# Top-k attention and a gated MLP: the place of a score copy in ScalarE's order, and the slots in which q and k are loaded and prepared

## The chip, the cores and the metric

The kernel runs on one core of a Trainium2 chip. Its engines are TensorE (matmuls, PE in the profile; weight loads are listed as PEld), VectorE (DVE), ScalarE (ACT), GpSimd (POOL) and SyncE (SP), which here issues nearly all DMAs. Each works through its own list of instructions in order, and semaphores hold an instruction until what it needs is there. The metric is the device time of one execution in microseconds (us).

## The reference: what is computed

```python
scores = 1/sqrt(64) * q @ k.T               # q, k, v: 8 batches, 8 heads, 576 x 64, fp32
kth    = 32nd largest of each row
scores = where(scores >= kth, scores, -1e9)
attn   = exp(scores - max) / (sum + 1e-9)
x      = (attn @ v), heads side by side     # 4608 x 512
h      = x @ w_in                           # 512 x 2048
out    = (h * sigmoid(1.702 * h)) @ w_out   # 2048 x 512
```

Scores of 576 columns for 36,864 rows (8 x 8 x 576), a cut at the 32nd largest of each row, softmax over what is left, values, and then an MLP with a gate on the 4608 rows of x.

## The kernel before

**Slots.** Attention is cut into 144 slots, 18 to a batch. A slot is 128 query rows for a pair of heads; a batch has four pairs of heads and four full blocks of 128 rows for each (16 slots), and the last 64 rows of two pairs share a slot (2 "ends" slots). Both heads of a slot lie side by side in tiles of 2 x 576.

**The way of one slot m**, by function and line:

- `scores(m)`, L295, PE: scores into two PSUM tiles `s_ps` (there are two such buffers, so one slot's scores fill both). `copy_scores(m)`, L307, ACT: scaled, into the SBUF tile `sc`. It frees `s_ps`.
- `pair_up(m)`, L336, DVE, and L339, L349, POOL: the larger (`greater`) and the smaller (`lesser`) of columns k and k + 288. `pair_up(m)` is the 15th operation of the search of slot m - 1.
- `find(m)`, DVE: the search for the 32nd largest, 23 operations: MAX8 (L366, 8 largest of 288) and MATCH_REPLACE8 (L369) on `greater`, then `pair_up(m + 1)`, then two MAX8, two MATCH_REPLACE8 and two MAX8 on `lesser`, a merge (L373) and the cut (L378).
- `mask(m)`, L423, ACT, two instructions: needs the cut, and drives all below it far down. `exps(m)`, L431, ACT: exponentials and their sums `den`. Both together are `exponentials(m)`.
- `invert(m)`, L439 and L441, DVE: 1 / den. It is put into the search of the next slot, `find(m + 1)`, after a numbered operation. `normalize(m)`, L454, POOL: two multiplications by it.
- `split(m)`, L490, ACT: the 32-bit exponentials as two planes of 16 bits, written over `sc`; a DMA (L492, SP) brings them to DRAM as `rows`. `turn_by_dma(m)`, L498, SP: a transposing DMA brings them back as `pt`.
- `values_at(m)`, L557, PE: `pt` times v, into the PSUM tile `o`. `x_of`, L571 (L574 for ends slots), ACT: into the resident x (`xT`). When a block of 128 rows has all its heads it is ready for the MLP.

**The MLP** has 36 blocks of 128 rows and goes in units of 512 columns of PSUM: `hidden` (L618, PE, into `ph`; four chunks of one block, "x 128", or two chunks of two blocks, "x 256"), `tanh` (L640 and a copy L643, ACT), `gate` (L652, L653, POOL), `project` (L673, PE, into `po`), and when a block has all 16 chunks an eviction `ob` (L681, ACT) and a DMA to the output. `hidden` does nothing when no block is ready.

**The order** is written out by hand. `opening` and `slot(n)` do slots 0 to 12 and round the weights to what the matmuls take. From slot 13 on, `two_slots(n)` (n odd) does two slots in one call, and after the last one `last_slot` does what is left of the MLP. This text calls one such call a pair. In `two_slots(n)` from n = 17 on, ScalarE gets, in this order:

1. `mask(n - 1)`, `exps(n - 1)`; in a preparing pair then the copy into halves (L246, below)
2. `tanh` of the first hidden unit, `split(n - 1)`
3. `mask(n)`, `copy_scores(n + 2)`, `exps(n)`, `x_of`, evictions
4. `copy_scores(n + 3)`, `split(n)`, `tanh` of the second unit, evictions

TensorE gets: hidden, project, `scores(n + 2)` ("first scores"), values of slots n - 3 and n - 2, `scores(n + 3)` ("second scores"), hidden, project. VectorE gets `find(n)` with `invert(n - 1)` in it, and `find(n + 1)` with `invert(n)` in it. Calls 13 and 15 put `scores(n + 2)` and its copy first.

**Loading and preparing q and k.** A table `later` holds what is due in which slot. For a pair of heads hp of batch b, `load` brings q (three DMAs on SP: L184 twice, L187) and k (three more) into one tile of two buffers. From batch 2 on `prepare_by_dma` has ScalarE copy them into 16-bit halves (L246; the tile comes from the pool that also holds the exponentials), four DMAs write them to DRAM (L250 twice, L254, L255), and a transposing DMA (L259, issued behind the one of L498) brings `qT` and `kT`. For batch 1 `prepare_by_pe` does it with transposes on PE: the main parts (L217, copied by ACT at L218), and as `second_part` the ends (`prepare_ends`, L222, copied at L223 and L225). These functions run only in the first slot of a pair, behind step 1 above. `FETCH` and `READY` give the slots of loading and preparing relative to the first slot of the batch, one number for each hp. v is loaded (`load_v`, L198, L206, three DMAs) in the slots `VALUES`.

In `two_slots`, the work of `todo[0]` that is not preparing is issued behind `split(n - 1)` and ahead of its transposing DMA; that of `todo[1]` behind `split(n)` and ahead of its own.

Of the kernel before, what the change touches and what calls it, by code (L numbers as in the profile page):

```python
# [30 lines left out]
def kernel(  # L31
# [250 lines left out]
    PER = N // B  # L282
# [61 lines left out]
    def pair_rest():  # L344

        while unpaired:
            n = unpaired.pop()
            whole, b = lesser[n][:].bitcast(I32), st[n]["sc"][:, :, HALF:S]
            nc.gpsimd.tensor_tensor(out=whole, in0=whole, in1=b.bitcast(I32), op=ALU.add)  # L349
# [44 lines left out]
    def lows(n):  # L394

        top, cut = st[n]["top"], st[n]["cut"]
        low = st[n]["low"] = small.tile([P, 2], F32, name="low")
        for i in range(2):
            nc.gpsimd.tensor_scalar(
                low[:, i : i + 1], cut[:, i : i + 1], top[:, i, TOPK : TOPK + 1], -1.0, op0=ALU.add, op1=ALU.mult  # L400
            )
# [11 lines left out]
    def exponentials(n, between=lambda: None):  # L413

        mask(n)
        between()
        exps(n)

    def mask(n):

        sc, cut = st[n]["sc"], st[n]["cut"]
        for i in range(2):
            nc.scalar.activation(sc[:, i, :], sc[:, i, :], AF.Prelu, bias=cut[:, i : i + 1], alpha=HUGE)  # L423

    def exps(n):

        sc, low = st[n]["sc"], st[n]["low"]
        pr = st[n]["pr"] = prp.tile([P, 2 * S], F32, name="pr")
        den = st[n]["den"] = small.tile([P, 2], F32, name="den")
        for i in range(2):  # L430
            nc.scalar.activation(  # L431
                pr[:, i * S : (i + 1) * S], sc[:, i, :], AF.Exp, bias=low[:, i : i + 1],
                accum_out=den[:, i : i + 1],
            )

    def invert(n):

        some = small.tile([P, 2], F32, name="some", tag="sums")
        nc.vector.tensor_scalar_add(some[:], st[n]["den"][:], 1e-9)  # L439
        rden = st[n]["rden"] = small.tile([P, 2], F32, name="rden", tag="inverse")  # L440
        nc.vector.reciprocal(rden[:], some[:])  # L441
# [158 lines left out]
    to_gate, gated, to_project = [], [], []  # L600

    def hidden(into=None):
        if not ready:
            return
        blocks = ready[:2]
        many = len(blocks)
        fs = blocks[0].left[: G // many]
        first, step = min(x.place for x in blocks), abs(blocks[0].place - blocks[-1].place) or 1
        blocks = sorted(blocks, key=lambda x: x.place)
        if many > 1 or pos["other"] or "ps_h" in in_use:  # L610
            pos["rest"] = 2
        elif pos["rest"]:
            pos["rest"] -= 1
        into = ps_t if pos["rest"] else into
        ph = (into or ps_h).tile([P, G * P], F32, name="ph", tag="tp" if into else "ph")
        for i, f in enumerate(fs):
            for c in range(CC):
                nc.tensor.matmul(  # L618
                    ph[:, i * many * P : (i + 1) * many * P],
                    lhsT=win[:, c, f * P : (f + 1) * P],  # L620
                    rhs=xs[:, first : first + step * (many - 1) + 1 : step, c, :],
                    start=(c == 0),
                    stop=(c == CC - 1),
                )
        to_gate.append((ph, fs, blocks))
        for x in blocks:
            x.left = [f for f in x.left if f not in fs]
        if many > 1:
            pos["other"] = True
        while ready and not ready[0].left:  # L630
            free.append(ready.pop(0).place)
            if len(ready) < 1 or len(ready[0].left) == FC:
                pos["other"] = False
# [13 lines left out]
    def gate(aside):  # L647
        if not gated:
            return
        th, h, g, blocks = gated.pop(0)  # L650
        if aside:
            nc.gpsimd.tensor_scalar(th[:], th[:], 1.0, 1.0, op0=ALU.add, op1=ALU.mult)  # L652
            nc.gpsimd.tensor_tensor(out=th[:], in0=th[:], in1=h[:], op=ALU.mult)  # L653
        else:
            nc.vector.scalar_tensor_tensor(
                out=th[:], in0=th[:], scalar=1.0, in1=h[:], op0=ALU.add, op1=ALU.mult
            )
        to_project.append((th, g, blocks))
# [43 lines left out]
    def at(n, fn, *args):  # L702
        later.setdefault(n, []).append((fn, args))
# [1 line left out]

    READY = (-13, -11, -5, -3)
    READY_1 = (-5, -3, -1, 1)
    FETCH = (-17, -15, -9, -7)  # L710
    FETCH_1 = (-11, -9, -4, -2)
    VALUES = (0, 1, 2, 3)
    by_slot = dict(enumerate([2, 2, 3, 3, 3, 3, 3, 3, 3, 3, 2, 2]))
# [11 lines left out]
            at(hp - 2, prepare, name, 0, hp)  # L725
    for b in range(1, B):
        for hp in range(NP):
            at(b * PER + (FETCH if b > 1 else FETCH_1)[hp], load_both, b, hp)
            if b > 1:
                at(b * PER + READY[hp], prepare_by_dma, b, hp)  # L730
            else:
                at(b * PER + READY_1[hp], prepare_by_pe, b, hp)
            at(b * PER + VALUES[hp], load_v, b, hp)
    unfinished = []
# [3 lines left out]
    def finish_one():  # L738
        unfinished.pop(0)()

    def may_project(waiting):

        return len(to_project) > waiting and len(finished) >= NG * CC + to_project[0][1][-1] + 1
# [62 lines left out]
    def bring_all():  # L806

        waiting = len(ready)
        while put_off:
            put_off.pop(0)()  # L810
        if len(ready) > waiting:
            hidden()
# [90 lines left out]
    def two_slots(n):  # L903

        preparing = prepare_by_dma, prepare_by_pe
        todo = [later.pop(m, []) for m in (n, n + 1)]
        live = lambda m: 0 <= m < N
        aside = n < N
        opens = n == SETTLED + 1
        ahead = n < SETTLED + 4  # L910
        assert not any(fn in preparing for fn, _ in todo[1])

        def begin(some):
            for fn, args in some:
                if fn not in preparing:
                    fn(*args)

        def prepare_some():
            for fn, args in todo[0]:
                if fn in preparing:  # L920
                    fn(*args)

        def find(m):
            for i, op in enumerate(topk_of_pairs(m) if live(m) else [lambda: None] * 23):
                op()
                if i == (20 if m % 2 else 18) and live(m - 1):
                    invert(m - 1)
                if i > 1 and unfinished:
                    finish_one()

        def measure(m):
            if live(m):
                lows(m)
            pair_rest()
            gate(aside)

        def project_one():
            if may_project(0):
                project(True)

        if opens:
            bounds(n - 1)
            gate(aside)
        if ahead:
            scores(n + 2)
        if opens:
            bring_all()
        if live(n - 1):
            exponentials(n - 1)
        if ahead:  # L950
            copy_scores(n + 2)
        if opens:
            leave_all()
            tanh(aside)
        prepare_some()
        hidden(ps_t if opens else None)
        while second_part:
            second_part.pop()()
        project_one()
        find(n)  # L960
        if live(n - 1):
            normalize(n - 1)
        tanh(aside)
        measure(n)
        if live(n - 1):
            split(n - 1)
        begin(todo[0])
        if live(n):
            mask(n)
        held = [m for m in (n - 3, n - 2) if live(m) and "rows" in st[m]]  # L970
        if live(n + 2) and not ahead:
            scores(n + 2)
            copy_scores(n + 2)
        o = ps_t.tile([P, 2, P], F32, name="o", tag="tp") if held else None
        for i, m in enumerate(held):
            values_at(m, o[:, i, :])
        if live(n - 1):
            turn_by_dma(n - 1)
        while turns:
            turns.pop(0)()  # L980
        if live(n + 3):
            scores(n + 3)
        if live(n):
            exps(n)
        if held:
            x_of(held, o)
        leave_all()
        hidden(ps_t)
        if live(n + 3):
            copy_scores(n + 3)  # L990
        find(n + 1)
        if live(n):
            normalize(n)
            split(n)
        begin(todo[1])
        if live(n):
            turn_by_dma(n)
        tanh(aside)
        measure(n + 1)
        project_one()  # L1000
        leave_all()
# [39 lines left out]
```

## Time and profile before

| | us |
|---|---|
| median of 3 runs (lowest, highest) | 1469.7 (1468.23, 1469.85) |
| the profiled execution | 1469.86 |
| its span, first to last instruction | 1468.0 |
| busy: PE, DVE, ACT, POOL | 1428.0, 1337.2, 1154.8, 970.8 |
| slots 13 to 143, by VectorE's searches | from 157.7 to 1396.7 |

The profile shows one execution. Its page gives the busy time of each engine, 40 slices of the span, the chain of work that ended last, and groups of instructions with their count, mean length and the idle time ahead of them. Behind the page stands the trace, which answers with waits (who waited for whom: us in total, times, longest), with a timeline (start, length, engine, line, operation, tiles and shapes, count of instructions merged; in brackets the idle time ahead and what ended it), and with the granted clock of TensorE for any stretch. Two things matter in reading it. Matmuls are pipelined and their ends modelled, so one matmul's row may overlap the next and a waiting TensorE can look busy: differences of starts are safer than lengths. And a float32 matmul has two rows.

Four ranges can be told apart: the opening and slots 0 to 12 (to about 158 us), pairs 13 to 19 with batch 1's preparation on PE (to about 231 us), the steady pairs of 18.8 to 19.8 us (to about 1397 us), and the rest of the MLP on PE, to the end.

### The profile page before, as it was taken

The numbers are of one execution on the slowest core, as the hardware profiler recorded it, in microseconds if no ns is written. First come the engines' busy times: TensorE is split into PE (matmuls) and PEld (weight loads), VectorE is DVE, ScalarE is ACT, GpSimd is POOL, SyncE is SP. The second block draws the span as 40 slices with busy tenths as digits, with TensorE's granted clock in tenths as the row PEclk, the third lists the DMA queues.
The fourth block names the chain that finished last, engine by engine and source line by source line (L and its number), as shares of the span: only waits on it lengthen the run. The fifth ranks groups of instructions, "written<-read, shape, count | busy, mean of one in ns | idle before, by whom it ended". The sixth has DMA issues, their size and how long they took to land. (4 is left out here: it accounts for less than half of the span.)

```text
span 1468.0 us, 29154 instructions
## 1 busy us (share of the span) xinstructions
PE 1428.0 (97%) x9564; PEld 1006.4 (69%) x9564; DVE 1337.2 (91%) x4672; ACT 1154.8 (79%) x1865; POOL 970.8 (66%) x1171
## 2 busy tenths in 40 slices
PE   7789989999999999999999999999999999999998
PEld 5667746777666667777666667777666667777665
DVE  7999999999999999999999999999999999999910
ACT  6998787878788887878888787888878787778730
POOL 3777666676676776666767667667677666677610
PEclk8899999999999999999999999999999999999999
DMA  7452266767677676776678676776768776644530
GB/s 220 142 156 73 64 169 172 203 170 190 160 196 191 181 176 181 199 183 171 173 189 191 180 180 169 203 185 173 186 175 189 179 192 169 165 131 130 136 88 15
DMA packets 516312, 242.04 MB, mean 165 GB/s; under 512 B 452672, under 2 KB 490560, under 8 KB 516160
## 3 DMA queue, kind: packets, MB, share of 16 engines
q1 hardware_dynamic: 515728, 239.89, 62.8%
q8 instruction: 75, 1.23, 0.4%
q14 instruction: 77, 0.63, 0.1%
q10 hardware_dynamic: 432, 0.30, 0.1%
HBM read 45.09 MB, written 102.24 MB: 100 GB/s over the span
## 5 line engine op out<-in xcount | busy, mean ns | idle before, releaser
L618 PEld LDWEIGHTS ph<-xT,win 128*128 128x128 f32 x3520 | 484.7, 191 | 89.0 <-issue 52.6
L618 PE MATMUL ph<-xT,win 128*128 128x128 f32 (+1 forms) x3520 | 538.0, 309 | 3.8 <-ACT xT L574 2.9
L673 PE MATMUL po<-wout,th 128*128 128x512 f32 x1152 | 522.3, 596 | 0.0
L490 ACT COPY sc<-pr 128x2304 uint16<-128x2304 uint16 x132 | 279.0, 2113 | 153.8 <-POOL pr L454 153.7
L673 PEld LDWEIGHTS po<-wout,th 128*128 128x128 f32 x1152 | 214.8, 192 | 214.5 <-issue 209.0
L366 DVE MAX8 top<-left 128x8 f32<-128x288 f32 x792 | 320.9, 446 | 0.0
L339 POOL TENSOR_TENSOR lesser<-sc,greater 128x576 int32<-128x576 int32 x132 | 186.3, 1411 | 195.2 <-DVE greater L336 194.5
L454 POOL TENSOR_SCALAR pr<-pr,rden 128x576 f32<-128x576 f32 x264 | 194.1, 748 | 125.8 <-DVE top L373 85.9
L369 DVE MATCH_REPLACE8 left<-top,left 128x288 f32<-128x288 f32 x528 | 229.6, 442 | 0.0
L431 ACT ACTIVATE pr<-sc,low 128x576 f32<-128x576 f32 x288 | 219.6, 767 | 0.0
L366 DVE MAX8 top<-lesser 128x8 f32<-128x288 f32 x528 | 213.7, 446 | 0.0
L423 ACT ACTIVATE sc<-sc,cut 128x576 f32<-128x576 f32 x288 | 207.4, 770 | 6.5 <-POOL cut L410 3.8
L295 PE MATMUL s_ps<-qk_t 64*128 64x288 f32 (+1 forms) x1280 | 190.3, 433 | 0.2 <-ACT qk_t L218 0.2
L349 POOL TENSOR_TENSOR lesser<-lesser,sc 128x576 int32<-128x576 int32 x132 | 186.5, 1413 | 0.2
L307 ACT ACTIVATE sc<-s_ps 128x576 f32<-128x576 f32 x288 | 170.3, 644 | 4.8 <-PE s_ps L295 3.4
L653 POOL TENSOR_TENSOR th<-th,h 128x512 f32<-128x512 f32 x129 | 165.3, 1282 | 10.8
L295 PEld LDWEIGHTS s_ps<-qk_t 64*128 64x128 f32 (+1 forms) x1280 | 106.2, 178 | 80.1 <-issue 57.8
L640 ACT ACTIVATE th<-ph 128x512 f32<-128x512 f32 x144 | 85.5, 594 | 76.0 <-PE ph L618 72.1
L557 PE MATMUL o<-pt,v_l 128*64 128x128 f32 (+1 forms) x2368 | 143.5, 264 | 0.0
L557 PEld LDWEIGHTS o<-pt,v_l 128*64 128x64 f32 x2368 | 119.8, 137 | 26.9 <-issue 18.4
L336 DVE TENSOR_TENSOR greater<-sc 128x576 f32<-128x576 f32 x132 | 99.8, 756 | 40.0 <-ACT sc L307 40.0
L652 POOL TENSOR_SCALAR th<-th 128x512 f32<-128x512 f32 x129 | 80.0, 620 | 57.7 <-ACT th L640 57.7
(78 smaller groups left out, 1386.6 us busy)
## 6 DMA issues: line engine op xcount, KB each, us to landing
rows<-sc SPq DMA_DIRECT2D x132, 576.0 KB, 3.2
qk_rows<-halves SPq DMA_DIRECT2D x48, 256.0 KB, 2.8
qk_l<-in_q_dram SPq DMA_DIRECT2D x64, 128.0 KB, 3.3
raw<-in_moe_w_in_dram SPq DMA_DIRECT2D x16, 512.0 KB, 4.6
v_l<-in_v_dram SPq DMA_DIRECT2D x32, 256.0 KB, 3.7
raw<-in_moe_w_out_dram SPq DMA_DIRECT2D x16, 512.0 KB, 3.5
out_dram<-ob SPq DMA_DIRECT2D x32, 256.0 KB, 2.9
qk_l<-in_k_dram SPq DMA_DIRECT2D x62, 128.0 KB, 3.0
```

What stands on the lines that cost most here:

```text
L295: nc.tensor.matmul(ps[i][rows, c, 0:HALF], lhsT=qT[b, hps[p]][on, cols], rhs=kT[b, hps[p]][on, FIRST[i] + c * HALF : FIRST[i] + (c + 1) * ...
L339: nc.gpsimd.tensor_tensor(out=whole, in0=a.bitcast(I32), in1=greater[n][:].bitcast(I32), op=ALU.subtract)
L349: nc.gpsimd.tensor_tensor(out=whole, in0=whole, in1=b.bitcast(I32), op=ALU.add)
L366: nc.vector.max(found(r, i, True), src[:, i, :])
L369: nc.vector.match_replace(to[:, i, :], found(r, i), src[:, i, :], LOWEST)
L423: nc.scalar.activation(sc[:, i, :], sc[:, i, :], AF.Prelu, bias=cut[:, i : i + 1], alpha=HUGE)
L431: nc.scalar.activation(pr[:, i * S : (i + 1) * S], sc[:, i, :], AF.Exp, bias=low[:, i : i + 1], accum_out=den[:, i : i + 1],)
L454: nc.gpsimd.tensor_scalar(pr[:, i, :], pr[:, i, :], st[n]["rden"][:, i : i + 1], 1.0, op0=ALU.mult, op1=ALU.mult)
L490: nc.scalar.copy(out=halves, in_=pr[:].bitcast(U16).rearrange("p (k h) -> p h k", h=2))
L557: nc.tensor.matmul(o[j * D : (j + 1) * D, cols], lhsT=main[:, j, c, :] if c < NF else tail[:, j, :], rhs=pt[:, MAIN[j] + c if c < NF else ...
L618: nc.tensor.matmul(ph[:, i * many * P : (i + 1) * many * P], lhsT=win[:, c, f * P : (f + 1) * P], rhs=xs[:, first : first + step * (many - ...
L673: nc.tensor.matmul(x.po[:], lhsT=gT[:, i * P : (i + 1) * P], rhs=wout[:, f, :], start=(x.done == 0), stop=(x.done == FC - 1))
```

## The change

ScalarE's step 3 becomes `copy_scores(n + 2)`, `mask(n)`, `exps(n)`: the copy of the first scores is issued ahead of the mask of the second slot. (In calls 13 and 15, where the copy stands earlier anyway, the order on ScalarE stays.)

`READY` goes from -13, -11, -5, -3 to -13, -9, -5, -1, so that between two preparing pairs there is always another pair. `FETCH` goes to -17, -15, -11, -7, and for batches from 2 on q is loaded in that slot and k in the next one (`FETCH[hp] + 1`, the second slot of the same pair). Batch 1 keeps its slots.

`invert(m - 1)` in `find(m)`: before, behind operation 20 for odd m (first slot of a pair) and 18 for even m. After, behind operation 18, and 20 only for even m in a pair in which something is prepared (`busy`). Between operations 18 and 20 stand two MAX8.

When the first `hidden` of a call had nothing to do, `project_one` runs ahead of `second_part` instead of behind it.

```diff
-    READY = (-13, -11, -5, -3)
+    READY = (-13, -9, -5, -1)
...
-    FETCH = (-17, -15, -9, -7)
+    FETCH = (-17, -15, -11, -7)
...
         for hp in range(NP):
-            at(b * PER + (FETCH if b > 1 else FETCH_1)[hp], load_both, b, hp)
             if b > 1:
+                for i, name in enumerate("qk"):
+                    at(b * PER + FETCH[hp] + i, load, name, b, hp)
                 at(b * PER + READY[hp], prepare_by_dma, b, hp)
             else:
+                at(b * PER + FETCH_1[hp], load_both, b, hp)
                 at(b * PER + READY_1[hp], prepare_by_pe, b, hp)
...
+        busy = any(fn in preparing for fn, _ in todo[0])
...
-                if i == (20 if m % 2 else 18) and live(m - 1):
+                if i == (20 if busy and m % 2 == 0 else 18) and live(m - 1):
                     invert(m - 1)
...
+        units = len(to_gate)
         hidden(ps_t if opens else None)
+        if len(to_gate) == units:
+            project_one()
         while second_part:
             second_part.pop()()
-        project_one()
+        if len(to_gate) > units:
+            project_one()
         find(n)
...
         begin(todo[0])
-        if live(n):
-            mask(n)
         held = [m for m in (n - 3, n - 2) if live(m) and "rows" in st[m]]
         if live(n + 2) and not ahead:
             scores(n + 2)
             copy_scores(n + 2)
...
         if live(n + 3):
             scores(n + 3)
         if live(n):
-            exps(n)
+            exponentials(n)
```

## The prediction

> **What bounds the kernel now.** I read the page's first part, then the waits by engine, then TensorE's own rows of one pair of slots in the timeline. The page leaves two candidates:
>
> ```profile
> PE 1428.0 (97%) x9564; PEld 1006.4 (69%) x9564; DVE 1337.2 (91%) x4672; ACT 1154.8 (79%) x1865; POOL 970.8 (66%) x1171
> ```
>
> The list of waits seems to name VectorE: once in every pair it stands still at `pair_up` until ScalarE has copied the first scores, and that is the copy which the change moves.
>
> ```profile
> DVE greater L336 <- ACT sc L307: 40.0, 63, 1.3
> ...
> DVE some L439 <- ACT pr L431: 9.1, 6, 6.3
> ...
> PE ph L618 <- ACT xT L574: 2.9, 4, 1.2
> ```
>
> If VectorE set the pace, 40 us were to be had. The timeline of TensorE speaks against it. This is the call for slots 75 and 76 (start in us, length, line, tile):
>
> ```profile
> 757.00 1.24 PE L295 MATMUL s_ps<-qk_t 64*128 64x288 f32 x8
> 758.17 1.09 PE L557 MATMUL o<-pt,v_l 128*64 128x128 f32 x16
> ...
> 760.50 1.24 PE L295 MATMUL s_ps<-qk_t 64*128 64x288 f32 x8
> 761.67 3.72 PE L618 MATMUL ph<-xT,win 128*128 128x256 f32 x16
> 765.23 3.60 PE L673 MATMUL po<-wout,th 128*128 128x512 f32 x8
> 768.67 3.62 PE L618 MATMUL ph<-xT,win 128*128 128x256 f32 x16
> 772.12 3.60 PE L673 MATMUL po<-wout,th 128*128 128x512 f32 x8
> 775.65 1.24 PE L295 MATMUL s_ps<-qk_t 64*128 64x288 f32 x8
> ```
>
> Ends are modelled here, so I read starts. From 757.00 to 775.65 is 18.65 us, and each step in it (1.17 for first scores to values, 2.33, 1.17, 3.56, 3.44, 3.45, 3.53) returns to within 0.005 us in dozens of pairs, which steps that wait on another engine would not. So 18.65 us is TensorE's own floor for a pair with two blocks in a unit; with one block the same steps sum to 18.89 us (662.24 to 681.09 is 18.85, 681.09 to 699.97 is 18.88). VectorE's pairs take 18.79 us (from the first MAX8 on `greater` of slot 77 at 764.11 to that of slot 79 at 782.90), of which 0.52 is the wait: its floor is 18.27. **TensorE is the bound, and VectorE's 40 us lie beside it**. TensorE also never rests after attention: from 1390 to 1460 us it is busy for all 70.0 us.
>
> What can be won is therefore only TensorE's own stalls. A stalled pair shows them as a longer step (first scores at 794.29, second scores here):
>
> ```profile
> 797.87 1.77 PE L295 MATMUL s_ps<-qk_t 64*128 64x288 f32 x8
> 799.57 1.78 PE L618 MATMUL ph<-xT,win 128*128 128x256 f32 x7
> ```
>
> From second scores to hidden this is 1.70 instead of 1.17. In the same way I went through all steps after 231 us. One round of two batches has excess of 0.48 (at 627.43), 0.60 (795.46 and 797.87), 0.23 (835.74), 0.15 (854.62), 0.45 (873.56), 0.14 (892.65) and 0.06 (912.85): 2.11 us. The rounds before and after repeat it to the hundredth, so 3 x 2.11 = **6.3 us**. Apart from these there is 0.94 at 362.66, 703.63 and 1044.59 and about 1.3 before 1386.29: there hidden waits for `x_of` of the ends block (the L574 line above).
>
> **The change, part by part.**
>
> *Copy ahead of mask.* ScalarE now, in the pair of 757.00:
>
> ```profile
> 755.75 2.11 ACT L490 COPY sc<-pr 128x2304 uint16<-128x2304 uint16 x1 [1.00 <-POOL pr L454]
> 757.77 1.44 ACT L423 ACTIVATE sc<-sc,cut 128x576 f32<-128x576 f32 x2
> 759.11 1.17 ACT L307 ACTIVATE sc<-s_ps 128x576 f32<-128x576 f32 x2
> 760.17 0.77 ACT L431 ACTIVATE pr<-sc,low 128x576 f32<-128x576 f32 x1
> ```
>
> The copy ends at 760.28, 0.22 before the second scores, which need its buffers; in the pair of 794.29 it ended at 798.35, after them. Nothing is added or removed. Behind the split the copy may start when the scores end, 757.00 + 1.24 = 758.24, and ends at 759.41: 1.1 us ahead of the second scores. Then mask at 759.30 (step 1.06), exponentials 760.64 (step 1.34), `x_of` 762.16 (step 1.52), its end 762.52 instead of 762.05. So the copy gains 0.87 and exponentials and `x_of` lose 0.47, since mask no longer fills the wait for the scores. For VectorE the wait of 0.52 at `pair_up` goes; it would come to `invert` (L439) at 762.63 - 0.52 = 762.11, and the sums are there at about 762.2. **The next wait is this one, 0.1 us or more**. It costs nothing while VectorE's floor plus it stays under TensorE's 18.65, that is up to 0.38 a pair. Bounds: 0, and 1.34 (all of mask). I take 0.1, the row's own arithmetic. Behind L439 queue two or four MAX8, then the next slot; for it waits POOL's normalize (1.47), the split (2.11), its rows (3.2 to land) and the transpose back (4.8). The transposes land 0.5 to 2.8 us before values need them, so a few tenths are covered.
>
> *invert.* In the first slot of a pair L439 moves ahead of two MAX8 (0.81): normalize and split come 0.7 earlier, which lets the copy start when the scores end. In the second slot of a preparing pair it moves 0.81 later; the cover there is the transposes' margin (0.6 to 1.6 us in such pairs).
>
> *Preparing in pairs that do not adjoin.* The 24 copies into halves (2.10 each) stay. Today half of them stand in a call that begins with an eviction `ob` (617.03, 693.07, 787.51, 863.12), and there the pair takes 19.25 to 19.77; a preparing pair without `ob` (770.50, 846.15) takes 18.80. The new slots (5, 9, 13, 17 of 18) miss the `ob` slots (3, 7, 11, 15). That removes the 0.48, 0.60 and 0.45 once more; the sum counts them once. Of the moved work each DMA counts: three issues for q and three for k, about 2 us each on SP, now stand in two gaps in which SP waits 3.2 us for rows to land anyway, where all six, behind three of v, filled one gap (757.89 to 765.41) and pushed the transpose behind. The pair's own transposed q and k (3.5 to 4.3 on SP) land a whole pair before their scores.
>
> *project ahead of prepare_ends.* Only in slots 17 and 19, where hidden has nothing. The output matmuls then fill the 3.2 and 3.9 us for which L222 waits on L218. The second time TensorE is back in the full sequence at 230.98. VectorE gains 0.81 at slot 14 (MAX8 in front of a waiting L439) and 0.52 in slots 17 and 19's pairs; so find(19) starts at 212.67 instead of 214.00, L439 at 220.27, normalize ends 222.3, split 224.4, then copy, mask, exponentials, `x_of` to 228.8. Hidden starts there instead of 230.98: 2.1 us. Against it, the granted clock fell to 0.74 of full in 214 to 223 us, and the output matmuls of 220.33 took 5.97 instead of 3.53, those of 202.02 4.89. The idle gap is now behind the output matmuls and the loss can fall on what follows: 0 to 2.4 us, I take the smaller of the two, 1.4. Net gain **0.7**, between -0.3 and 2.1.
>
> *Ends.* `x_of` in the three ends pairs: first scores + 5.55 instead of 5.71, gain 0.5. At the last one (1386.25) there was no preparing, so it is 0.6 later: a loss.
>
> Sum: 6.3 + 0.7 + 0.5 - 0.6 = 6.9 us. The profiled execution took 1469.86 (span 1468.0 and 1.86 around it), 0.16 over the median of 1469.7; so 1463.0, and 1462.8 beside the median.
>
> [...]
>
> [...]
>
> **Rivals.**
> 1. *VectorE is the bound.* For: 40.0 us of waits, 0.52 in nearly every pair. Against: the pair of 18.65 without slack in TensorE. Time about 1430. Chance 0.03.
> 2. *More goes*: the waits for `x_of` shrink and the clock holds at the start: 2.1 instead of 0.7 there and up to 2.8 at the ends, 1458 to 1460. Chance 0.12.
> 3. *The stalls only change places.* The 6.3 us come back as later transposes or late copies, in pairs with `ob`: there exponentials of the slot before end 3.3 us ahead of the first scores, and L439 (now earlier) waits some 0.7 for them. If normalize and split then end over 1.1 us after the earliest copy, second scores stall again. About 1468, range 1466.8 to 1472.6. Chance 0.14.
> 4. *Slower: mask now stands on VectorE's path.* Place: L439 in the second slot of each pair, behind copy and mask. Price: 1.34 at most on each of about 63 pairs. VectorE's pair is then 18.27 + wait, and it decides against the mean pair of today (18.94 from slot 21 to 141) when the wait is over 0.67; fully exposed, 0.67 x 63 = 42 us, so 1473 to 1512. For: exponentials really end 0.47 later and VectorE comes there 0.52 sooner. Against: those two meet within 0.1 us. Chance 0.08.
>
> The forecast itself, 1460.0 to 1466.7, has 0.63.
>
> **How the numbers follow.** A measurement can tell about 0.2% (2.9 us) from no change. Faster by more than that: 0.63 + 0.12 + 0.03 = 0.78. Within: 0.14. Slower: 0.08. Low end 1459.0: the forecast with the start's full 2.1 and most of the ends' wait. High end 1468.0: the forecast with all bounds against it (no gain at the start, half the stalls back) and the larger part of rival 3. Left out: rival 1, rival 4, the outer parts of 2 and 3, together 0.2.
>
> **What would show it.** Right: VectorE's waits at L336 nearly gone and those at L439 grown to some 0.1 to 0.4 a pair; first scores 18.65 or 18.89 apart in all pairs, preparing ones too; second scores to hidden 1.17 everywhere but at the ends; output matmuls before L222 in slots 17 and 19. Wrong: pairs of VectorE near 18.3 (rival 1), transposes landing after 19.8 us from their first scores (rival 3), L439 waiting 0.7 or more in every pair (rival 4).

## The result, and the profile after

The changed kernel takes 1469.09 us (median of 12 runs, 1467.94 to 1470.5), the kernel before 1468.92 in its 12 runs (1467.73 to 1470.11). The ratio is 1.0001, with a 95% interval of 0.9992 to 1.001: no difference that can be measured, where 1462.8 was forecast. The profiled execution took 1469.48 us (span 1467.7).

The page's first part, after:

```profile
PE 1426.2 (97%) x9564; PEld 1002.1 (68%) x9564; DVE 1350.5 (92%) x4672; ACT 1160.3 (79%) x1865; POOL 970.6 (66%) x1171
```

The waits after, VectorE's first and then TensorE's (us in total, times, longest):

```profile
DVE some L439 <- ACT pr L431: 33.1, 32, 6.4
...
DVE greater L336 <- ACT sc L307: 0.8, 3, 0.3
```

```profile
PE ph L618 <- ACT xT L571: 4.2, 16, 0.7
PE ph L618 <- ACT xT L574: 4.0, 4, 1.9
```

VectorE's 40.0 us at `pair_up` are gone (0.8 left), and only 24 of them came back at `invert` (9.1 to 33.1). The time did not move. So those waits did lie beside TensorE's work. The new line is TensorE's first, the third of the four: the hidden matmuls now wait for `x_of` of the ordinary blocks (L571), 16 times; before, only for that of the ends blocks (L574). 4.2 us is less than what it costs, since matmul ends are modelled; the starts tell more. Below, T is the start of a pair's first scores. This is TensorE in a pair before (T = 567.21) and the same pair after (T = 564.58):

```profile
570.71 1.24 PE L295 MATMUL s_ps<-qk_t 64*128 64x288 f32 x8
571.88 3.90 PE L618 MATMUL ph<-xT,win 128*128 128x128 f32 x32
575.62 3.60 PE L673 MATMUL po<-wout,th 128*128 128x512 f32 x8
```

```profile
568.09 1.24 PE L295 MATMUL s_ps<-qk_t 64*128 64x288 f32 x8
569.26 0.71 PE L618 MATMUL ph<-xT,win 128*128 128x128 f32 x4
570.19 3.39 PE L618 MATMUL ph<-xT,win 128*128 128x128 f32 x28 [0.22 <-ACT xT L571]
573.42 3.60 PE L673 MATMUL po<-wout,th 128*128 128x512 f32 x8
```

Before, the unit took 575.62 - 571.88 = 3.74 us; after, 573.42 - 569.26 = 4.16. It now falls in two: four rows run, then TensorE stands, then the other 28 run. The four rows are the first two of the four slices of x (each matmul has two rows). The block was finished in this very pair: the pair's `x_of` writes its last two slices, and the third matmul needs them. At 3.675 / 32 = 0.115 us a row it was due at 569.26 + 0.46 = 569.72, T + 5.14. ScalarE says when they came:

```profile
565.85 1.19 ACT L307 ACTIVATE sc<-s_ps 128x576 f32<-128x576 f32 x2 [1.10 <-PE s_ps L295]
566.93 1.44 ACT L423 ACTIVATE sc<-sc,cut 128x576 f32<-128x576 f32 x2
568.26 0.77 ACT L431 ACTIVATE pr<-sc,low 128x576 f32<-128x576 f32 x1
...
569.78 0.36 ACT L571 COPY xT<-o 128x256 f32<-128x256 f32 x1
570.03 1.20 ACT L307 ACTIVATE sc<-s_ps 128x576 f32<-128x576 f32 x2
```

The copy (L307) starts at T + 1.27 and stands ahead of mask (L423), as ordered. `x_of` ends at 570.14, T + 5.56, and 0.05 later TensorE goes on. In the same pair before, the row was

```profile
571.98 0.35 ACT L571 COPY xT<-o 128x256 f32<-128x256 f32 x1
```

and ended at 572.33, T + 5.12: already 0.06 too late (the unit took 3.74 instead of 3.675, which is its floor, the time that it takes in pairs without a stall).

Pair by pair, the steps of starts give the whole balance. Of one round (18 pairs, from the pair at 359.01 before):

| us per round | before to after |
|---|---|
| second scores to hidden returns to 1.17 (once to 1.13; in the 0.60 are 0.07 of the values) | -0.48 -0.60 -0.13 -0.23 -0.15 -0.45 -0.14 = -2.18 |
| hidden behind `x_of`, pair with ends | -0.15 |
| hidden stalls, one-block pairs in which a block is finished | +0.43 +0.49 +0.43 +0.49 = +1.84 |
| hidden stalls, two-block pairs (3.63 or 3.67 instead of 3.56) | +0.07 +0.07 +0.11 +0.07 = +0.32 |
| sum | -0.17 |

Over the whole execution, cut at the scores of the pair of slot 21 and 59 pairs later (us; "tail" ends with the last matmul). The last column is the median less the two middle columns and 5.7 (the profiled time less the end of PE, 1469.86 - 1464.16). It is an estimate of what the first part takes in the median run, on the assumption that the rest takes what it takes in the profile.

| kernel | first part, profile | 59 pairs | tail | first part, by the median |
|---|---|---|---|---|
| before | 245.19 | 1117.25 | 101.72 | 244.3 |
| after | 243.15 | 1117.79 | 102.86 | 242.7 |

The tail's 1.14 is one more stall of 0.49 and the last ends block: its hidden starts 4.44 instead of 3.80 after the start of the values ahead of it.

### The profile page after: what moved, and what is told of

It is laid out like the page before. It is cut to its first block, busy times and chain, and to the rows that moved or that the text cites. A ratio compares the mean times of both kernels' runs of the same rounds, so it can differ in the third digit from the quotient of the medians.

```text
span 1467.7 us, 29137 instructions
## 1 busy us (share of the span) xinstructions
PE 1426.2 (97%) x9564; PEld 1002.1 (68%) x9564; DVE 1350.5 (92%) x4672; ACT 1160.3 (79%) x1865; POOL 970.6 (66%) x1171
## 4 chain that ended last, share of the span: by engine, by line
PE 84%; DVE 7%; ACT 6%; issue 2%; SPq 0%; POOL 0%; DMA 0%; ACTq 0%; POOLq 0%; DVEq 0%
PE ph L618 34%; PE po L673 32%; PE s_ps L295 9%; PE o L557 7%; DVE top L317 3%; DVE left L320 2%; ACT sc L307 2%; ACT pr L431 2%; ACT sc L423 1%; PE tp L468 1%; DVE top L366 1%; PE o L526 1%; DVE left L369 0%; PE none L169 0%; DVE win L152 0%
## 5 line engine op out<-in xcount | busy, mean ns | idle before, releaser
L307 ACT ACTIVATE sc<-s_ps 128x576 f32<-128x576 f32 x288 | 171.9, 652 | 60.0 <-PE s_ps L295 59.7
L423 ACT ACTIVATE sc<-sc,cut 128x576 f32<-128x576 f32 x288 | 207.3, 774 | 7.5 <-POOL cut L410 4.8
L295 PE MATMUL s_ps<-qk_t 64*128 64x288 f32 (+1 forms) x1280 | 184.1, 434 | 0.2 <-ACT qk_t L218 0.2
L295 PEld LDWEIGHTS s_ps<-qk_t 64*128 64x128 f32 (+1 forms) x1280 | 100.1, 179 | 78.7 <-issue 53.6
L369 DVE MATCH_REPLACE8 left<-top,greater 128x288 f32<-128x288 f32 x264 | 114.8, 443 | 0.0
```

What stands on the lines that cost most here:

```text
L295: nc.tensor.matmul(ps[i][rows, c, 0:HALF], lhsT=qT[b, hps[p]][on, cols], rhs=kT[b, hps[p]][on, FIRST[i] + c * HALF : FIRST[i] + (c + 1) * ...
L307: nc.scalar.mul(out=to, in_=ps[i][:, :, 0:HALF], mul=SCALE)
L369: nc.vector.match_replace(to[:, i, :], found(r, i), src[:, i, :], LOWEST)
```

## The experiments

Theory A: the changed order of ScalarE loses what the rest wins, through one thing only, that `x_of` ends later, at T + 5.56 (by 0.44 in the pair shown), while hidden needs it at T + 5.14. Against it stand two others: that the gain is lost elsewhere (the new waits at L439, later transposes, late copies) and `x_of` only shows it; and that the other three parts win nothing. In the expectations A is always theory A.

The kernel before was run again beside the experiments, in three series with medians of 1468.22, 1468.58 and 1468.27. The ratios below are to the series beside them; differences in us are to the 1468.92 and 1469.09 of the result and can be off by some 0.7.

**1. `x_of` early** (the changed kernel with `x_of` ahead of the exponentials, so that copy and mask alone stand before it):

```diff
         if live(n):
-            exponentials(n)
+            mask(n)
         if held:
             x_of(held, o)
+        if live(n):
+            exps(n)
```

> The changed kernel with one step moved: x_of is issued ahead of the exponentials of slot n instead of behind them (copy, mask, x_of, exponentials). Theory A (x_of came 0.5 to 0.7 us later and hidden, whose third chunk needs it, waits): x_of ends about 4.1 us after the first scores' start instead of 5.56, and all of hidden's stalls go: 15 of 0.49, some 1.0 in pairs with two blocks, 0.79 at three ends pairs, most of the last, and 1.0 at the start. That is 11 to 13 us off the changed kernel, about 1457. Theory B (VectorE's grown wait for the exponentials at L439 sets the pace): the exponentials come another 0.25 us later in each of 63 pairs, so no gain, 1469 to 1485, and L439's wait grows in step with the time.

Measured: 1457.06 us, ratio 0.992 [0.9906, 0.9933]. The same pair, TensorE and then ScalarE (T = 563.34):

```profile
566.85 1.24 PE L295 MATMUL s_ps<-qk_t 64*128 64x288 f32 x8
568.02 3.84 PE L618 MATMUL ph<-xT,win 128*128 128x128 f32 x32
571.69 3.60 PE L673 MATMUL po<-wout,th 128*128 128x512 f32 x8
```

```profile
565.69 1.44 ACT L423 ACTIVATE sc<-sc,cut 128x576 f32<-128x576 f32 x2
567.02 0.37 ACT L571 COPY xT<-o 128x256 f32<-128x256 f32 x1
567.27 0.79 ACT L431 ACTIVATE pr<-sc,low 128x576 f32<-128x576 f32 x1
```

`x_of` ends at 567.39, T + 4.05, before hidden starts, and the unit takes 571.69 - 568.02 = 3.67: the floor. This holds for hidden in all pairs from slot 21 on; the 59 pairs take 1108.20. Exponentials now end at T + 5.57, 0.27 later than after, and the kernel is 12 us faster: the theory that the gain is lost elsewhere falls.

**2. Mask first again** (the changed kernel with the old place of mask, the other three parts kept):

```diff
         begin(todo[0])
+        if live(n):
+            mask(n)
         held = [...]
...
-            exponentials(n)
+            exps(n)
```

> The changed kernel with the order on ScalarE put back (mask of slot n ahead of the copy of the first scores); invert, the spread and project stay as changed. Theory A: x_of ends 4.2 to 5.1 us after the first scores' start, as it did before the change, so the 0.49 stalls go while the other parts keep the copy early enough for the second scores: 8 to 10 us under the changed kernel, 1459 to 1461. Theory C (TensorE's stalls only change places whatever the order): 1467 to 1471. Theory B: faster too, by as much as L439's wait shrinks (33 us in the changed kernel), 1445 to 1460.

Measured: 1457.21, ratio 0.9923 [0.991, 0.9937], better than expected (1459 to 1461). `x_of` ends at T + 4.2 to 5.03, the second scores do not stall, and the 59 pairs take 1107.85. So the theory that the other parts win nothing falls: they win 11.7 us (1468.92 - 1457.21), and the copy ahead of mask costs 11.9 (1469.09 - 1457.21).

**3. The copy alone** (the kernel before with the copy ahead of mask and nothing else):

```diff
         begin(todo[0])
-        if live(n):
-            mask(n)
         held = [...]
...
-            exps(n)
+            exponentials(n)
```

> The kernel before with only the copy of the first scores put ahead of the mask. Theory A: the stalls of the second scores behind the copy (6.3 us) go, but x_of ends at least 5.56 us after the first scores' start in every pair, so that 15 pairs stall 0.5, some 1.0 comes in pairs with two blocks and 0.6 at the last: 1 to 3 us slower than before, 1469.5 to 1471.5, with no step of second scores to hidden over 1.2 outside the ends pairs. Theory D (the copy ahead is what wins, and the other parts lose it): 5 to 7 us faster.

Measured: 1472.43, ratio 1.0025 [1.0014, 1.0035], 0.9 above the range expected by A. The stalls of hidden are those of after to the hundredth (4.16 and 4.20; 3.63 and 3.67), and the old stalls of second scores are gone too. The 59 pairs take 1118.23 and the tail 102.85, 2.1 together over before; the other 1.4 fall to the first part by the median (245.7 against 244.3), though in the profiles it takes 245.22 and 245.19. Why stays open.

**4. `x_of` early in the kernel before:**

```diff
-        if live(n):
-            exps(n)
         if held:
             x_of(held, o)
+        if live(n):
+            exps(n)
```

> The kernel before with x_of ahead of the exponentials, nothing else. Theory A: before the change x_of was late only in the three ends pairs (0.94 each) and at the last one (about 1.3 of it partly to be had), so 3 to 4 us off, 1465 to 1466; the stalls behind the late copy (6.3 us) stay. Theory C: no difference, within 1.5 us of before.

Measured: 1469.42, ratio 1.0004 [0.9995, 1.0012]: a miss. The ends pairs gained: hidden starts at T + 5.15 instead of 5.76. But the gain was given back in the pairs behind them:

```profile
383.10 1.37 PE L295 MATMUL s_ps<-qk_t 64*128 64x288 f32 x8
384.40 3.72 PE L618 MATMUL ph<-xT,win 128*128 128x256 f32 x16
```

Second scores to hidden is 384.40 - 383.10 = 1.30 here, and 1.30 to 1.32 in each of the four pairs behind the ends, where the kernel before has 1.17. These pairs are 18.78 to 18.79 long. VectorE waits 0.52 at `pair_up` in each: the round from its search over mask and the late copy back to its next search takes 18.79, longer than TensorE's 18.65. In the kernel before, as I read the same steps, the 0.94 lost at the ends lets VectorE get ahead, and the pairs of 18.65 behind it live on that at 0.14 each (there the end of `x_of` moves from T + 4.76 over 4.90 and 5.05 to 5.20). So the ends' stall in that kernel was partly the price of a round that the copy sets, and its removal by `x_of` alone brings little. That is not the whole of the miss: the 59 pairs (1116.56) and the tail (100.95) are together 1.5 shorter than before, and the first part is 2.0 longer by the median (246.2 against 244.3). Why the first part is longer stays open.

**5. `x_of` late** (the changed kernel with `x_of` behind the copy of the second scores):

```diff
+        if live(n + 3):
+            copy_scores(n + 3)
         if held:
             x_of(held, o)
         leave_all()
         hidden(ps_t)
-        if live(n + 3):
-            copy_scores(n + 3)
```

> A dose test: the changed kernel with x_of later still, behind the copy of the second scores (two instructions, 1.1 us). Theory A: every pair whose second hidden takes a block just finished (about 30 of them) stalls 1.1 us longer, so 25 to 36 us over the changed kernel, about 1495 to 1505. Theory B or C: the exponentials keep their time, so VectorE's waits do not grow at first; 1469 to 1473.

Measured: 1504.97, ratio 1.0246 [1.0232, 1.026]. The waits:

```profile
PE ph L618 <- ACT xT L571: 32.4, 28, 1.9
PE ph L618 <- ACT xT L574: 7.3, 4, 1.9
```

Where a block is finished, hidden takes 5.25 in most one-block pairs (4.16 after) and 4.71 in most two-block pairs (3.63 after), 1.08 to 1.09 more: past its cover, what `x_of` loses is paid in full, at every block that is finished.

**6 to 8. One part each in the kernel before.** The spread preparation and loads (`READY` and `FETCH` of the change's diff):

> The kernel before with only the new slots of loading and preparing. Theory A: no preparing pair begins with an eviction any more, so the stalls of 0.48, 0.60 and 0.45 go in each of three rounds; pairs with two blocks stay at VectorE's 18.79 instead of TensorE's 18.65, which gives some 0.7 a round back: 4 to 6 us faster, 1462 to 1465. Theory D: within 1.5 us of before.

Measured: 1462.16, ratio 0.9955 [0.9941, 0.9968]; the 59 pairs take 1109.91, and in the three ends pairs that had the 0.94 the step from second scores to hidden falls from 2.11 to 1.30. The places of invert:

```diff
-                if i == (20 if m % 2 else 18) and live(m - 1):
+                if i == (20 if busy and m % 2 == 0 else 18) and live(m - 1):
```

> The kernel before with only the new places of invert. Theory A: split and copy come 0.7 earlier in ordinary pairs, so VectorE's wait at L336 and the small stalls (0.06 to 0.23) go; in the pairs with both a preparation and an eviction ScalarE is busy up to the split, not waiting, so 0.48, 0.60, 0.45 and the 0.94 at the ends stay: 1 to 3 us faster, 1465.5 to 1467.5. Theory D: within 1 us of before or slower.

Measured: 1466.69, ratio 0.9984 [0.9975, 0.9993]; 59 pairs 1114.83, with 0.48, 0.53, 0.45 (preparing pairs that begin with `ob`) and 0.93 (ends) left of each round. The move of project:

```diff
+        units = len(to_gate)
         hidden(ps_t if opens else None)
+        if len(to_gate) == units:
+            project_one()
         while second_part:
             second_part.pop()()
-        project_one()
+        if len(to_gate) > units:
+            project_one()
```

> The kernel before with only project ahead of prepare_ends in slots 17 and 19. Theory A: TensorE reaches the steady pairs up to 2 us earlier, but VectorE and the copy do not come earlier, and second scores wait for the copy: 0 to 1 us faster, 1467.3 to 1468.5. Were TensorE alone the bound from there on: 2 us faster, 1466.

Measured: 1470.6 (1468.0 to 1472.25), ratio 1.0014 [1.0006, 1.0023]: a miss. Its profiled execution is the fastest of its 11 runs; in it the first part takes 243.56, 1.6 less than in the profile of before (whose 1469.86 lies above its median), and the pairs are as before but for 0.2. By the median the first part is 1.9 longer (246.2 against 244.3).

**9. Mask first and `x_of` early** (the second experiment with `x_of` ahead of the exponentials):

```diff
-            exps(n)
+            pass
         if held:
             x_of(held, o)
+        if live(n):
+            exps(n)
```

> Mask back ahead of the copy and x_of ahead of the exponentials, the other three parts kept. Theory A (the changed order loses only through the late end of x_of, and the other three parts gain some 11.5 us): the steady pairs already stood at TensorE's floor with mask first alone (1457.2), so nothing is left there, and only the ends are to be had: 3 x 0.13 at the ends pairs and about 0.5 at the last one. 1456 to 1457, x_of's end below first scores + 4.6 in all pairs. Rival B (the place of the copy itself costs or brings something beside x_of): over 2 us away from the run with x_of early and the copy ahead (1457.1), on one side or the other.

Measured: 1458.17 (1455.51 to 1461.21), ratio 0.9928 [0.9916, 0.9941]. 59 pairs and tail are the shortest of all (1107.44 and 100.95), as A has it; the eleventh below has the same two figures. The time is 1.2 above the range expected by A, with 1.1 us between this run and the first experiment, but its first part is longer, 244.1 by the median and 247.17 in the profile. The three kernels at 1457 to 1458 cannot be told apart: their intervals overlap.

**10 and 11. Is the move of project worth anything?** Spread and invert without it, on the kernel before; and the first experiment without it.

> Before, with the spread loads and preparation and the new places of invert, without the move of project and without the copy ahead. Alone they gave 6.5 and 2.2 us, beside one another they remove partly the same stalls. If the move of project is worth the 2.0 us by which slot 21 began earlier in the profile after: 1459 to 1460. If it is worth nothing, as its run alone said (1470.6 against 1468.6): 1457 to 1458.

Measured: 1460.41, ratio 0.9943 [0.9931, 0.9956]; 59 pairs and tail are those of the second experiment to the hundredth (1107.85, 101.72). The time is 0.4 above the range for a move that is worth 2.0.

> The changed kernel with x_of ahead of the exponentials (1457.1 on the chip), and project put back behind the ends' transposes. Same question as for the run beside it, from the other side: about 1459 if the move of project brings 2 us, 1457 if nothing, 1455 if it costs what its run alone showed.

Measured: 1458.56, ratio 0.9933 [0.992, 0.9947], nearest to the 1459 of a move that brings 2 us.

All the first parts, by the median: with the move of project 242.7 (after), 242.2 (first experiment), 241.9 (second), 244.5 (fifth), 244.1 (ninth) and 246.2 (eighth); without it 244.3 (before), 245.7 (third), 246.2 (fourth), 244.8 (sixth), 244.4 (seventh), 245.1 (tenth) and 244.5 (eleventh). Together with the spread and the new invert it brings 1.5 to 3.2 us in the medians (1458.56 - 1457.06 and 1460.41 - 1457.21), though the intervals of these pairs of kernels overlap, so that a gain is likely but not shown. Alone it costs 1.7 (1470.6 - 1468.92). Why the two differ stays open.

## Why the prediction was wrong, point by point

**The step that failed** is in "Copy ahead of mask": it worked out rightly that exponentials and `x_of` lose 0.47, and priced the loss at VectorE's next wait and, under "Ends", at the last ends block alone (0.6). `x_of` in the steady pairs was costed at nothing, and the cover was never named. The cover was hidden's first two slices of x, to T + 5.14 in a one-block pair, and in the one-block pairs that finish a block `x_of` before the change ended at up to T + 5.12. What it missed: 15 stalls that grew by 0.42 to 0.53 and 12 of 0.07 to 0.11, together 8.0 us (7.0 + 1.0), against the 6.5 that the end of the old stalls brought. Nor did it ask what `x_of` would be without the new order. Against the second experiment, which lacks that order alone, the change loses 7.5 and 1.0 at these blocks, 2.0 in the three ends pairs that had the 0.94 before (the step from second scores to hidden is 1.96 instead of 1.30 or 1.31) and 0.65 at the last ends block: 11.1 of the 11.9. The rest lies in the first part. The first, second and fifth experiments show it from three sides: the stall goes when `x_of` is earlier, by either way, and grows with it when it is later.

The trace of before had the sign. The 0.06 at 912.85, which the prediction listed among the stalls to be removed, is hidden's own wait for `x_of` (its unit takes 3.74 instead of 3.675). It was read as one stall more of the old kind, where it was an operation at the edge of its cover.

**The bound: right.** TensorE sets the pace; the floors of 18.65 and 18.89 are met within 0.04 in every ordinary pair of the first experiment from 263.42 on (pairs with ends have 0.15 more of values). One correction: in the kernel before, the round over the copy, 18.79, is the limit of a two-block pair once TensorE no longer stalls (fourth experiment). The change (and, by the earlier normalize, invert and spread without the copy) takes that away. Rival 1 held VectorE, with its 40.0 us of waits at `pair_up`, for the bound; 39 of them went and the time stayed.

**Copy, and the next wait.** The copy came at T + 1.27 (forecast 1.24), `x_of`'s end at T + 5.56 (forecast 762.52 - 757.00 = 5.52), the wait at L336 went. The wait at L439 was forecast at 0.1 or more in every pair; from slot 21 on it came as 1.1 to 1.4 in nearly all one-block pairs that begin with an `ob`, as 0.2 to 0.8 in four of the two-block pairs of a round, and as less than 0.1 in the others. It cost nothing: in the one-block stretches VectorE's pairs alternate between 18.17 and 20.09 us, in the mean 19.13, which is TensorE's pace (18.89 and 19.37 in turn).

**invert, and preparing in pairs that do not adjoin: 6.3 us.** It came, as 3 x 2.18 = 6.5 (the list had left out the step of 1.26 at 817.04, 0.13, and counted the 0.06 at 912.85). But it has more than one cause that suffices: the copy alone, or spread with invert, removes the same stalls (third and tenth experiments). Since the others had removed them already, the copy ahead of mask had nothing left to win in the steady pairs and only its price to pay.

**Project: 0.7.** Perhaps undersized: the first part is shorter by 2.0 in the profiles and by 1.6 by the medians (244.3 - 242.7), inside the bounds of -0.3 to 2.1. How much of that is the move's own is not shown: alone it is a loss. The loss by the clock, put at 1.4, does not show in the profiles: over 190 to 240 us the granted clock is 0.93 after and 0.90 before.

**Ends: +0.5, -0.6.** Measured +0.45 and -0.64. But the spread alone, in the sixth experiment, gains 0.81 in each of these three ends pairs; under the new order only 0.15 of it is left.

**The rivals.** The time is that of rival 3 (about 1468), and so is its heading, stalls that only change places. Its mechanism was another: it named later transposes and late copies in pairs with `ob`, and second scores do not stall anywhere after. Rival 4 had the right operation to blame, mask, but on VectorE's path; mask stood on the path to `x_of`.

## What to carry to other kernels

When an operation is moved up in an engine's list, everything that it passes is later by a sum that can be worked out; for each of these, name the consumer, when it needs the result, and the margin in the trace, also for a small copy of 0.36 us at the end of the list. A wait of some hundredths that shows in only a few pairs is not noise: here it was the place where the margin was used up, and from there a delay cost its full length each time. When several parts of a change remove the same stall, price each one as the last to be added.

## What the runs showed that was not expected

The first part's length differs by up to 5 us between executions with nearly the same work, and the granted clock goes with it: over 200 to 235 us it is 0.85 or 0.86 in four of ten profiles (before, third, ninth and eleventh experiment), whose first parts take 245.19 to 247.17, and 0.90 or 0.95 in the other six (after, first, second, seventh, eighth and tenth), with 241.78 to 245.20. Between 110 us and the end of TensorE's work, the profile of before has half clock in two stretches only, of 3.4 us from 201.3 and of 6.8 us from 218.4, with full clock for 13.7 us between them; the profile after has it in one, of 6.8 us from 207.8. In the eighth experiment 6.8 us of it begin at 205.8, in the ninth at 228.4. The ninth experiment and then the second, where TensorE is idle in part, near 227 us (columns: stretch; us; busy time of PE, PEld, DVE, ACT, POOL; granted clock; DMA share; GB/s):

```profile
225.00:228.40 3.40, 1.65 (x25) 1.27 (x22) 3.40 (x14) 3.40 (x5) 0.97 (x1) 0.99 0.49 160
228.40:235.20 6.80, 6.80 (x28) 5.74 (x28) 6.73 (x25) 4.44 (x9) 4.08 (x6) 0.50 0.65 154
```

```profile
223.90:227.30 3.40, 2.65 (x28) 1.78 (x24) 3.40 (x13) 3.40 (x7) 0.00 (x0) 1.00 0.74 245
227.30:230.70 3.40, 3.40 (x29) 3.21 (x29) 3.33 (x14) 1.85 (x5) 2.08 (x2) 1.00 0.48 112
```

In the ninth, TensorE is busy for 1.65 of 3.4 us, and the 6.8 us behind them run at half clock (0.50); in the second it is busy for 2.65 of 3.4, and the clock stays at 1.00. Half clock (0.50 over 6.8 us) also came behind 1.26 of 3.5 us before (from 214.90), 1.11 of 3.4 after (from 204.40) and 1.73 of 3.8 in the eighth (from 202.00). What sets the clock these profiles do not show. The first part ends at 247.17 in the ninth and at 241.78 in the second. So a change at the start can be judged only by medians of several runs, and a single profile of it may be off by more than the gain.
